# Far groups' softmax sums with a constant column, an early load of the softplus table, and another order up to the first MLP's end

## Chip, cores, metric

The kernel runs on one core of one Trainium2 chip. The metric is the device time of one execution in microseconds. For a profiled execution the span is also known: the time from the program's first instruction to its last.

## What is computed

Three stages follow each other: attention in a window of 64 positions, a softplus MLP, and a gated MLP.

```python
batch, n_heads, seq, head_dim = (4, 8, 576, 64)
scores = scale * np.matmul(q, k.transpose(0, 1, 3, 2))
mask = (rel >= 0) & (rel < window)          # rel = pos[:, None] - pos[None, :], window = 64
scores = np.where(mask, scores, -1000000000.0)
attn = np.exp(scores - np.max(scores, axis=-1, keepdims=True))
attn = attn / (np.sum(attn, axis=-1, keepdims=True) + 1e-09)
x = np.matmul(attn, v)                      # to 2304 tokens x 512
h = x @ w_in                                # 512 x 2048
g = np.maximum(h, 0.0) + np.log1p(np.exp(-np.abs(h)))
x = g @ w_out                               # 2048 x 512
gate = 1.0 / (1.0 + np.exp(-(x @ w_gate)))  # 512 x 1536
out = (gate * (x @ w_val)) @ w_out2         # 1536 x 512
```

The weights and the second MLP's input come as 64-bit numbers and are used as pairs of rounded fp32 parts, a high and a low one; so are all activations that enter a matmul.

## The kernel before

**Groups.** The 2304 tokens are cut into 36 groups of 64 queries. For each, `att_scores` multiplies queries and keys on TensorE, `att_max` (VectorE) takes each row's maximum, `att_exp` (ScalarE, line 381) the exponential with a running sum of each row, `att_sum` (VectorE, lines 384 to 390) adds 1e-9 to the sums and takes the reciprocal, `att_norm` (GpSimd, line 397) multiplies, and then the result is transposed (on TensorE, lines 409 and 413, or for later groups by VectorE and DMAs) and multiplied with the values (`att_values`, line 474). `att_hi` (ScalarE, line 482) and `att_lo` (VectorE, line 487) write the high and low part of the attention output into the first MLP's input `xt`. Groups 0 to 7 are called near: they run before the first MLP starts, and are block 0. Groups 8 to 35 are far: they run while the first MLP works on the block before theirs.

**Sums.** In a near group the exponential's running sum goes into the first of two columns of a tile `sums` whose second column was set to 1e-9, and one `tensor_reduce` over the two columns adds it. In a far group it goes into the group's statistics tile `st`, and a `tensor_scalar` adds 1e-9:

```python
        if g < NG0:
            nc.vector.tensor_reduce(out=st[:, 1, :], in_=sums[:, g], axis=AX.X, op=ALU.add)
        else:
            nc.vector.tensor_scalar(out=st[:, 1, :], in0=st[:, 1, :], scalar1=1e-9, scalar2=None, op0=ALU.add)
```

**The first MLP, M1.** Five blocks of 512, 384, 384, 512 and 512 tokens; in each, 16 steps f. `m1_proj(b, f)` (line 514, 12 matmuls) projects into one of two PSUM banks h0 and h1. `m1_act` (ScalarE, line 531) is the softplus, in place. `g_hi` (ScalarE, line 538) and `g_lo` (VectorE, line 544) write its high and low part; after `g_lo` the bank is free, and `m1_proj(b, f + 2)` may use it. `m1_out(b, f)` (lines 491 to 493, 12 matmuls) adds into four other banks, two steps behind. In the text "the first projection" is `m1_proj(0, 0)`, "the third" `m1_proj(0, 2)`, and so on. The first two projections use all high parts first. ScalarE needs one table of functions for the exponential and another one for softplus; a load of a table stands in the program where the next activation needs another one than the last (`ACT_TABLE_LOAD`).

**Weights.** While block 0 runs, the first MLP's weights are turned from 64 bits into pairs, tile by tile: `w_load` (a DMA on SyncE's queue), `w_scale` (ScalarE, lines 175 and 177), `w_shift`, `w_sign`, `w_low` (VectorE, lines 181, 186, 191), `w_hi` (ScalarE, line 197) and `w_lo` (VectorE or GpSimd, line 205). Tiles 0 and 1 are the first two projections' weights; from tile 2 on, two tiles are scaled together. With the exponential's table in, `w_scale` uses another function (line 175), and `w_sign` isn't needed.

**The order.** All steps up to the first MLP's end are put into one list by a planner, `lead_in` (lines 1080 to 1167). Each step has an engine, a cost in us, the steps it depends on and a due time (`traits`, lines 903 to 1057, and lines 1082 to 1106). The planner keeps a time for each engine, and takes, again and again, from the steps that can start soonest (within `NEAR` or `SLACK`) the one that is due first. The numbers at the file's head steer it: `LATE` and `STAY` hold a visit of the attention on TensorE back or keep visits of a kind together, `SWITCH` and `FLIP` price a change of ScalarE's table, `FETCH` and `PAUSE` model the DMAs, `RG` spaces the near groups, `OPEN` is the planned start of the first MLP, `COMBO0` the slot at which the second MLP's weights are first prepared. The list fixes the order of instructions on every engine, the DMA queue of SyncE among them. What comes after the first MLP (lines 1178 to 1180) has an order of its own.

Of the kernel before, what the change touches and what calls it, by code (L numbers as in the profile page):

```python
# [10 lines left out]
F32 = mybir.dt.float32  # L11
# [3 lines left out]
AF = mybir.ActivationFunctionType  # L15
ALU = mybir.AluOpType
AX = mybir.AxisListType
# [3 lines left out]
P = 128  # L21
# [1 line left out]
HALF = 384  # L23
LAG = 2
LEAD = 7
COMBO0, COMBO = 37, 10.0
FAR = 2
MERGE = 8
SHIFTED = 2,
RG = 1.2  # L30
HURRY = 1.5
SLACK, NEAR = 0.1, 0.2
STAY = 10.0
FETCH, PAUSE, SAFE = 15.5, 1.4, 0.4
OPEN = 30.0
FLYING, SWITCH, MARGIN, FLIP, LATE = 10, 1.3, 1.1, 8, 0.5
EITHER, HALVES = (("pool", 1.29), ("dve lock", 0.69)), (("pool", 0.75), ("dve lock", 0.42))
COPIES = ("act", 0.55), ("dve", 0.69)
LO_AT = ((5, 2), (6, 6), (8, 9), (9, 12), (13, 15), (15, 18), (19, 21))
# [13 lines left out]
def tile_kernel(ctx: ExitStack, tc: tile.TileContext, qk, vt, w1, w2, wg, wv, wo, out):  # L53
# [20 lines left out]
    nc = tc.nc  # L74
# [19 lines left out]
    main = ctx.enter_context(tc.tile_pool(name="main", bufs=2))  # L94
# [6 lines left out]
    early = main.tile([P, 2, DM], BF16, tag="sums", name="early", bufs=1)  # L101
    ident16, mask16 = (early[:, k, :P] for k in range(2))
    sums = early[:, 0, P:2 * P].bitcast(F32).rearrange("p (g j two) -> p g j two", j=4, two=2)
    x2d = dram.tile([KC, P, NT], F32, tag="x2d", name="x2d")
    wcd = [dram.tile([P, 14 * HC], F32, tag=f"wcd{f}", name=f"wcd{f}") for f in range(NF2)]
    pd = [dram.tile([4, 32, 4, P], F32, tag=f"pd{i}", name=f"pd{i}") for i in range(2)]
# [155 lines left out]
    NG0 = BLOCKS1[0] // Q  # L262
# [107 lines left out]
    def att_bias(g, engine):  # L370
        t = st_t[g][:, 0, :]
        eng = nc.gpsimd if engine == "pool" else nc.vector
        eng.tensor_scalar(out=t, in0=t, scalar1=SCALE, scalar2=None, op0=ALU.mult)

    def att_exp(g):
        w = width(g)
        p, st = p_t[g], st_t[g]
        s, scale = ([p[:, j] for j in range(NPAIR)], 1.0) if g >= NG0 else (
            [s_t[g][:, h, j] for h in range(s_t[g].shape[1]) for j in range(NPAIR // s_t[g].shape[1])], SCALE)
        for j in range(NPAIR):  # L380
            nc.scalar.activation(out=p[:, j, :w], in_=s[j][:, :w], func=AF.Exp, bias=st[:, 0, j:j + 1], scale=scale,  # L381
                                 accum_out=sums[:, g, j, :1] if g < NG0 else st[:, 1, j:j + 1])

    def att_sum(g):
        st = st_t[g]
        if g < NG0:
            nc.vector.tensor_reduce(out=st[:, 1, :], in_=sums[:, g], axis=AX.X, op=ALU.add)
        else:
            nc.vector.tensor_scalar(out=st[:, 1, :], in0=st[:, 1, :], scalar1=1e-9, scalar2=None, op0=ALU.add)
        nc.vector.reciprocal(out=st[:, 2, :], in_=st[:, 1, :])  # L390

    def att_norm(g):
# [135 lines left out]

    def m1_act(b, f):
        t = h_t.pop((b, f))  # L530
        nc.scalar.activation(out=t, in_=t, func=AF.Softplus)  # L531
        u_t[b, f] = t

# [254 lines left out]
    for b in range(1, NB1):  # L788
        s0, s1 = pos[m1_proj, b - 1, 0], pos[m1_proj, b, 0]
        ng, g0 = BLOCKS1[b] // Q, starts1[b] // Q  # L790
        for j in range(ng):
            far = b >= FAR
            first = -5 if far else 5
            t = s0 + first + (s1 - s0 - (14 if far else 12 + first)) * (j // 2) // max(ng // 2 - 1, 1)
            attention(g0 + j, t, far)
            at(t - 4, -60, qk_load, g0 + j)

# [21 lines left out]
    for f in range(NF2):  # L819
        t, i = COMBO0 + int(COMBO * f), len(seq1) + 2 * f  # L820
# [12 lines left out]
    for f in range(NF2):  # L833
        i = WO_AT + f
        t = end + (-7, -1)[f] if f < 2 else pos[m2_out, 0, f - 2, 0] - 1
# [33 lines left out]

    def consts():  # L870
        nc.gpsimd.memset(sums, 1e-9)
        make_identity(nc, ident)
        nc.vector.tensor_copy(out=ident16, in_=ident)
        for t, inside, outside in (mask16, 0.0, -1e30), (mask, 3.0e38, -1e9):
            nc.gpsimd.memset(t, inside)
            for h in range(2):
                m = t[h * Q:(h + 1) * Q, :]
                nc.gpsimd.affine_select(out=m, in_=m, pattern=[[1, P]], compare_op=ALU.is_ge, fill=outside, base=-1,
                                        channel_multiplier=-1)
                nc.gpsimd.affine_select(out=m, in_=m, pattern=[[-1, P]], compare_op=ALU.is_ge, fill=outside, base=Q,  # L880
                                        channel_multiplier=1)
# [198 lines left out]
    def lead_in():  # L1080
# [30 lines left out]
        while todo:  # L1111
            ready, other = [], "soft" if table == "exp" else "exp"
            for n, key in enumerate(todo[:AHEAD]):
# [5 lines left out]
                if all(d in done for d in deps + after[key]):  # L1119
                    ends_at, best = [(done[d] - lead(key, d), made[d]) for d in deps], None  # L1120
                    visit = kind == "pe" and key[0] not in (m1_proj, m1_out) and key[1] >= NG0
                    for kind, us in kind if kind in CHOICES else ((kind, us),):
                        engine, *need = kind.split()
                        start = max([t - (0.08 if e == "pe" else 0.05) * (e == engine) for t, e in ends_at], default=0.0)
                        start = max(free[engine], start + LATE * visit)
                        if engine == "pool" or "lock" in need:
                            start = max(start, held["dve" if engine == "pool" else "pool"])
                        if engine == "sp" and len(flying) >= FLYING:
                            start = max(start, flying[-FLYING])
                        if engine == "act" and need and need[0] != table:  # L1130
                            us += SWITCH
                        if best is None or start + us < best[0] + best[2]:
                            best = start, kind, us
# [97 lines left out]
```

## Time and profile before

| | |
|---|---|
| time, median of 3 runs (range) | 878.88 us (878.85 to 881.1) |
| profiled execution | 878.93 us, its span 877.1 us |
| TensorE matmuls, busy | 868.3 us (99%) |
| TensorE weight loads, busy | 775.3 us (88%) |
| VectorE, ScalarE, GpSimd, busy | 519.4 us (59%), 395.5 us (45%), 151.1 us (17%) |
| 16 DMA engines | 202 GB/s to and from HBM over the span |

An engine's busy time counts its instructions from start to end; matmuls overlap and their ends are modelled. The engines wait for each other by semaphores, and each takes its own instructions strictly in order, so an instruction that waits holds up all behind it on its engine.

### The profile page before, as it was taken

Reading aid. Unit: us, or ns where it says so; the run is one execution under the profiler, and the core shown is the slowest. Engines: PE = TensorE matmul, PEld = TensorE weight load, DVE = VectorE, ACT = ScalarE, POOL = GpSimd, SP = SyncE. Lnnn points to the kernel's source line nnn. Section 1 sums busy time; section 2 is a strip of 40 time slices with the busy share of each in tenths; the row PEclk is TensorE's granted clock in tenths of the full one; section 3 lists DMA queues with packets and bytes.
Section 4 is the critical chain, followed back from the end, with each engine's and each line's share of the span. In section 5 each row is a group of like instructions: output and inputs, shape, how many; then the busy total and the mean of one; then the engine's idle time right before and its main releaser. Section 6 shows DMA issues by size and latency. Waiting matters only on the chain.

```text
span 877.1 us, 14033 instructions
## 1 busy us (share of the span) xinstructions
PE 868.3 (99%) x5307; PEld 775.3 (88%) x5307; DVE 519.4 (59%) x926; ACT 395.5 (45%) x870; POOL 151.1 (17%) x156
## 2 busy tenths in 40 slices
PE   8999999999999999999999999999999999999998
PEld 5787889999999888888889999999999999999997
DVE  5999985547665654555326677667444448444444
ACT  7878766556566763344323333343222225212222
POOL 5001110112000220012002232332111111111110
PEclk9999999999999999999999999999999999999999
DMA  9955647756877747643325755546554445444442
GB/s 363 390 181 207 207 143 269 246 207 211 263 254 261 266 150 269 199 165 132 133 84 208 269 207 216 217 168 240 208 200 160 151 150 209 168 158 168 169 168 73
DMA packets 56563, 177.73 MB, mean 203 GB/s; under 512 B 6128, under 2 KB 21744, under 8 KB 51888
## 3 DMA queue, kind: packets, MB, share of 16 engines
q1 hardware_dynamic: 56496, 176.84, 56.4%
q8 instruction: 42, 0.69, 0.3%
q14 instruction: 25, 0.20, 0.1%
HBM read 139.59 MB, written 37.22 MB: 202 GB/s over the span
## 4 chain that ended last, share of the span: by engine, by line
PE 93%; ACT 3%; DVE 3%; issue 1%; DMA 1%; POOL 0%; SPq 0%; POOLq 0%; DVEq 0%; ACTq 0%
PE h L514 21%; PE acc L491 11%; PE acc L492 11%; PE acc L493 11%; PE h L491 10%; PE h L493 10%; PE h L492 10%; PE at L493 2%; PE at L492 2%; PE at L491 2%; PE at L474 2%; PE at L335 1%; ACT w L381 1%; DMA w<-in_qk 1%; DVE w L186 1%
## 5 line engine op out<-in xcount | busy, mean ns | idle before, releaser
L514 PE MATMUL h<-xt,w 128*128 128x512 f32 (+1 forms) x960 | 211.6, 369 | 0.9 <-DVE g L544 0.7
L620 DVE TENSOR_TENSOR w<-h,w 128x384 f32<-128x384 f32 x216 | 117.1, 556 | 159.9 <-PE h L493 157.0
L514 PEld LDWEIGHTS h<-xt,w 128*128 128x128 f32 x960 | 174.2, 188 | 25.6 <-DVE g L544 0.9
L491 PE MATMUL h<-w,wc 128*128 128x384 f32 x504 | 169.1, 336 | 0.1
L493 PE MATMUL h<-w,wc 128*128 128x384 f32 x504 | 168.9, 335 | 0.0
L492 PE MATMUL h<-w,wc 128*128 128x384 f32 x504 | 168.7, 335 | 0.0
L632 POOL TENSOR_TENSOR g<-w,g 128x384 fp32r<-128x384 f32 x70 | 74.0, 1057 | 297.0 <-ACT g L625 252.1
L491 PE MATMUL acc<-g,w 128*128 128x512 f32 (+1 forms) x320 | 119.4, 373 | 0.0
L492 PE MATMUL acc<-g,w 128*128 128x512 f32 (+1 forms) x320 | 117.7, 368 | 0.0
L493 PE MATMUL acc<-g,w 128*128 128x512 f32 (+1 forms) x320 | 117.7, 368 | 0.0
L544 DVE TENSOR_TENSOR g<-h,g 128x512 fp32r<-128x512 f32 (+1 forms) x80 | 50.8, 636 | 93.9 <-ACT g L538 87.5
L531 ACT ACTIVATE h<-h 128x512 f32<-128x512 f32 (+1 forms) x80 | 43.0, 540 | 124.2 <-PE h L514 122.2
L491 PEld LDWEIGHTS h<-w,wc 128*128 128x128 f32 x504 | 94.6, 188 | 2.7 <-DVE w L620 0.7
L492 PEld LDWEIGHTS h<-w,wc 128*128 128x128 f32 x504 | 94.6, 188 | 2.0
L493 PEld LDWEIGHTS h<-w,wc 128*128 128x128 f32 x504 | 94.6, 188 | 0.0
L625 ACT CAST g<-w 128x384 fp32r<-128x384 f32 x72 | 36.9, 513 | 118.6 <-DVE w L620 118.6
L491 PEld LDWEIGHTS acc<-g,w 128*128 128x128 f32 x320 | 60.1, 188 | 8.9 <-issue 1.0
L493 PEld LDWEIGHTS acc<-g,w 128*128 128x128 f32 x320 | 60.1, 188 | 7.6
L492 PEld LDWEIGHTS acc<-g,w 128*128 128x128 f32 x320 | 60.1, 188 | 7.1
L397 POOL TENSOR_TENSOR p<-p,st 128x512 f32<-128x512 f32 x28 | 30.7, 1099 | 201.0 <-DVE st L390 114.4
L658 ACT ACTIVATE w<-w 128x384 f32<-128x384 f32 x36 | 19.0, 527 | 94.5 <-DVE w L620 94.4
L493 PE MATMUL acc<-w,g 128*128 128x512 f32 x144 | 56.9, 395 | 0.0
(138 smaller groups left out, 1187.6 us busy)
## 6 DMA issues: line engine op xcount, KB each, us to landing
wc<-wcd SPq DMA_DIRECT2D x36, 1792.0 KB, 7.3
qk<-in_qk SPq DMA_DIRECT2D x28, 512.0 KB, 5.5
wcd<-raw SPq DMA_DIRECT2D x24, 512.0 KB, 3.2
w<-in_w SPq DMA_DIRECT2D x16, 512.0 KB, 8.8
raw<-in_w SPq DMA_DIRECT2D x16, 512.0 KB, 4.9
v<-in_vt SPq DMA_DIRECT2D x25, 256.0 KB, 3.2
raw<-in_wg SPq DMA_DIRECT2D x12, 512.0 KB, 5.3
raw<-in_wv SPq DMA_DIRECT2D x12, 512.0 KB, 6.2
```

The costliest lines, as they stand in the source:

```text
L397: nc.gpsimd.tensor_tensor(out=p[:, j:j + n, :w], in0=p[:, j:j + n, :w], in1=st[:, 2, j:j + n].unsqueeze(2).to_broadcast([P, n, w]), op=ALU ...
L474: nc.tensor.matmul(out=o[h * Q:(h + 1) * Q, j, k * Q:(k + 1) * Q], lhsT=v[r, (2 * j + h) * Q:(2 * j + h + 1) * Q], rhs=pt, start=True, sto ...
L491: nc.tensor.matmul(out=o, lhsT=lh, rhs=rh, start=first, stop=False)
L492: nc.tensor.matmul(out=o, lhsT=lh, rhs=rl, start=False, stop=False)
L493: nc.tensor.matmul(out=o, lhsT=ll, rhs=rh, start=False, stop=last)
L514: nc.tensor.matmul(out=o, lhsT=w[:, i, kc * P:(kc + 1) * P], rhs=x[:, j, kc, :n], start=t == 0, stop=t == len(turns) - 1)
L531: nc.scalar.activation(out=t, in_=t, func=AF.Softplus)
L544: nc.vector.tensor_tensor(out=g[:, 1, :n], in0=t, in1=g[:, 0, :n].bitcast(F32), op=ALU.subtract)
L620: nc.vector.tensor_tensor(out=out, in0=a, in1=b, op=op)
L625: nc.scalar.copy(out=g[:, 0, :HALF], in_=t)
L632: eng.tensor_tensor(out=g[:, 1, :HALF], in0=t, in1=g[:, 0, :HALF].bitcast(F32), op=ALU.subtract)
L658: nc.scalar.activation(out=sb, in_=u2, func=AF.Sigmoid)
```

## The change

Three things are changed. The far groups' running sums go into a new tile `far_sums` of three rows (group g uses row g mod 3) with a second column of 1e-9, and all groups take their sum by `tensor_reduce`. The softplus table is asked for by an instruction of its own ahead of the first softplus. The planner's numbers are other ones; it counts on 0.135 us instead of 0.05 by which a step may start before its forerunner on the same engine is done, and gives the first softplus a start that is earlier by `SWITCH`; visits in the first MLP's blocks are due at slightly other slots.

```diff
-COMBO0, COMBO = 37, 10.0
+COMBO0, COMBO = 36, 10.0
-RG = 1.2
+RG = 1.0
-SLACK, NEAR = 0.1, 0.2
-STAY = 10.0
-FETCH, PAUSE, SAFE = 15.5, 1.4, 0.4
-OPEN = 30.0
-FLYING, SWITCH, MARGIN, FLIP, LATE = 10, 1.3, 1.1, 8, 0.5
+SLACK, NEAR = 0.1, 0.1
+STAY = 30.0
+FETCH, PAUSE, SAFE = 12.8, 1.4, 0.4
+OPEN = 35.0
+FLYING, SWITCH, MARGIN, FLIP, LATE = 10, 1.3, 1.1, 10, 1
...
+    far_sums = main.tile([P, 3, 4, 2], F32, tag="far_sums", name="far_sums", bufs=1)
...
+    def sum_row(g):
+        return sums[:, g] if g < NG0 else far_sums[:, g % 3]
+
...
-                                 accum_out=sums[:, g, j, :1] if g < NG0 else st[:, 1, j:j + 1])
+                                 accum_out=sum_row(g)[:, j, :1])
...
-        if g < NG0:
-            nc.vector.tensor_reduce(out=st[:, 1, :], in_=sums[:, g], axis=AX.X, op=ALU.add)
-        else:
-            nc.vector.tensor_scalar(out=st[:, 1, :], in0=st[:, 1, :], scalar1=1e-9, scalar2=None, op0=ALU.add)
+        nc.vector.tensor_reduce(out=st[:, 1, :], in_=sum_row(g), axis=AX.X, op=ALU.add)
...
+        if b + f == 0:
+            nc.scalar.preload_act_table(AF.Softplus)
         nc.scalar.activation(out=t, in_=t, func=AF.Softplus)
...
-            first = -5 if far else 5
-            t = s0 + first + (s1 - s0 - (14 if far else 12 + first)) * (j // 2) // max(ng // 2 - 1, 1)
+            first = -5 if far else 6
+            t = s0 + first + (s1 - s0 - (15 if far else 12 + first)) * (j // 2) // max(ng // 2 - 1, 1)
...
         nc.gpsimd.memset(sums, 1e-9)
+        nc.gpsimd.memset(far_sums, 1e-9)
...
-                        start = max([t - (0.08 if e == "pe" else 0.05) * (e == engine) for t, e in ends_at], default=0.0)
-                        start = max(free[engine], start + LATE * visit)
+                        start = max([t - (0.08 if e == "pe" else 0.135) * (e == engine) for t, e in ends_at], default=0.0)
+                        start = max(free[engine], start + LATE * visit - SWITCH * (key == (m1_act, 0, 0)))
```

What it does to the order is shown at three places, in the names of the program: `xt` is the first MLP's input, `bits` and `w` are weights, `h` a projection's bank, `g` the parts of its softplus. Line numbers of the changed kernel are higher by one to four.

ScalarE at the end of the near groups, before: the casts of groups 6 and 7 are the row with x2, and the first softplus is the row before the last.

```order
L482 CAST xt<-at 128x4x64
L197 CAST w_481<-bits 128x512
L443 COPY pt<-s_473 128x256
L175 ACTIVATE bits<-w_154 128x512
L482 CAST xt<-at 128x4x64 x2
L175 ACTIVATE bits<-w_255 128x1024
L197 CAST w_481<-bits 128x512
L175 ACTIVATE bits<-w_289 128x1024
L531 ACT_TABLE_LOAD
L531 ACTIVATE h_523<-h_523 128x512
L197 CAST w_566<-bits 128x2x512
L538 CAST g<-h_523 128x512
```

The same place now:

```order
L483 CAST xt<-at 128x4x64
L198 CAST w_483<-bits 128x512
L444 COPY pt<-s_475 128x256
L176 ACTIVATE bits<-w_156 128x512
L483 CAST xt<-at 128x4x64
L176 ACTIVATE bits<-w_257 128x1024
L483 CAST xt<-at 128x4x64
L198 CAST w_483<-bits 128x512
L176 ACTIVATE bits<-w_327 128x1024
L533 ACT_TABLE_LOAD
L534 ACTIVATE h_529<-h_529 128x512
L541 CAST g<-h_529 128x512
```

The scaling of weight tiles 2 and 3 (128x1024) moved between the casts of groups 6 and 7, the table load belongs to a line of its own, and the g cast moved ahead of a weight cast.

VectorE from the low half of weight tiles 4 and 5 on, before:

```order
L191 SCALAR_TENSOR_TENSOR bits<-w_289,bits 128x1024
L205 TENSOR_TENSOR w_566<-bits,w_566 128x512
L544 TENSOR_TENSOR g<-h_523,g 128x512
L205 TENSOR_TENSOR w_566<-bits,w_566 128x512
L205 TENSOR_TENSOR w_592<-bits,w_592 128x512 x2
```

and now:

```order
L192 SCALAR_TENSOR_TENSOR bits<-w_327,bits 128x1024
L547 TENSOR_TENSOR g<-h_529,g 128x512
L206 TENSOR_TENSOR w_571<-bits,w_571 128x512 x2
L365 SCALAR_TENSOR_TENSOR p<-at,mask 128x256
L364 MEMSET p 128x2x64
```

The subtraction for the first projection's g (`g_lo`) moved ahead of the low part of weight tile 2, and the maximum of group 8 follows the tiles 2 and 3.

ScalarE around the exponentials of groups 8 and 9, before (the fourth projection's softplus is the third row, the fifth one's the last):

```order
L177 ACTIVATE w_619<-raw 128x1024
L197 CAST w_670<-bits 128x2x512
L531 ACTIVATE h_650<-h_650 128x512
L381 ACT_TABLE_LOAD
L381 ACTIVATE p,st<-p,st 128x128 x4
L538 CAST g<-h_650 128x512
L381 ACTIVATE p,st<-p,st 128x128 x4
L197 CAST w_717<-w_619 128x2x512
L531 ACT_TABLE_LOAD
L531 ACTIVATE h_693<-h_693 128x512
```

and now:

```order
L178 ACTIVATE w_670<-w_508 128x1024
L534 ACTIVATE h_651<-h_651 128x512
L541 CAST g<-h_651 128x512
L178 ACTIVATE w_670<-w_566 128x1024
L198 CAST w_714<-w_627 128x2x512
L385 ACT_TABLE_LOAD
L385 ACTIVATE p,far_sums<-p,st 128x128 x8
L198 CAST w_760<-w_627 128x2x512
L534 ACT_TABLE_LOAD
L534 ACTIVATE h_692<-h_692 128x512
```

The exponentials moved behind the fourth projection's g cast and behind the scaling of tiles 12 and 14 (the two rows with w_670), which stood after the fifth softplus before. On TensorE the transposes of groups 8 and 9 moved from behind `m1_out(0, 4)` to ahead of the seventh projection, and the scores of groups 10 and 11 from behind the eighth projection to ahead of it; the transposes of groups 10 and 11 stand behind one `m1_out` more.

## Rows read from the trace of the kernel before

**Rows 1.** The page, part 1: busy us, share of the span, instructions.

```profile
PE 868.3 (99%) x5307; PEld 775.3 (88%) x5307; DVE 519.4 (59%) x926; ACT 395.5 (45%) x870; POOL 151.1 (17%) x156
```

**Rows 2.** Stretches: PE, PEld, DVE, ACT, POOL busy us (instructions); PEclk, DMA share, GB/s.

```profile
28.00:80.00 52.00, 50.67 (x310) 40.97 (x309) 49.62 (x75) 43.50 (x79) 4.93 (x4) 1.00 0.75 273
80.00:160.00 80.00, 80.00 (x584) 70.06 (x584) 63.15 (x104) 53.95 (x116) 8.53 (x8) 1.00 0.57 195
```

**Rows 3.** Order of time, TensorE, 23.5 to 35: start, us, instruction, [idle before <-releaser].

```profile
24.18 0.82 PE L504 MATMUL s<-idle 128*128 128x512 bf16 x2
25.14 0.70 PE L514 MATMUL h<-xt,w 128*128 128x512 f32 x2
...
30.77 0.90 PE L335 MATMUL at<-qk 64*64 64x128 f32 x32
32.41 2.79 PE L514 MATMUL h<-xt,w 128*128 128x512 f32 x11 [0.74 <-DVE g L544]
```

**Rows 4.** Order of time, TensorE, 59.5 to 77.

```profile
59.75 1.03 PE L413 MATMUL at<-ident,p 128*128 128x128 f32 x8
60.54 3.18 PE L514 MATMUL h<-xt,w 128*128 128x512 f32 x12
63.65 0.56 PE L335 MATMUL at<-qk 64*64 64x128 f32 x12
...
74.47 0.60 PE L413 MATMUL at<-ident,p 128*128 128x128 f32 x4
75.66 0.66 PE L413 MATMUL at<-ident,p 128*128 128x128 f32 x4 [0.59 <-POOL p L397]
76.07 1.18 PE L514 MATMUL h<-xt,w 128*128 128x512 f32 x4
```

**Rows 5.** The chain of work that ended last: start, us, engine and line.

```profile
81.79 2.72 PE h L514 x12
...
153.62 0.83 PE at L335 x32
...
321.32 2.94 PE h L514 x12
```

**Rows 6.** Order of time, ScalarE, 21.5 to 33.

```profile
24.00 0.65 ACT L482 CAST xt<-at 128x256 fp32r<-128x256 f32 x2
24.55 1.16 ACT L175 ACTIVATE bits<-w 128x1024 f32<-128x1024 f32 x1
...
28.20 1.28 ACT L531 ACT_TABLE_LOAD   x1 [0.52 <-PE h L514]
29.49 0.58 ACT L531 ACTIVATE h<-h 128x512 f32<-128x512 f32 x1
...
30.92 0.59 ACT L538 CAST g<-h 128x512 fp32r<-128x512 f32 x1
```

**Rows 7.** Order of time, VectorE, 24 to 33.

```profile
28.99 1.23 DVE L191 SCALAR_TENSOR_TENSOR bits<-w,bits 128x1024 uint32<-128x1024 uint32 x1
31.06 0.69 DVE L205 TENSOR_TENSOR w<-bits,w 128x512 fp32r<-128x512 f32 x1 [0.84 <-ACT w L197]
31.67 0.68 DVE L544 TENSOR_TENSOR g<-h,g 128x512 fp32r<-128x512 f32 x1
```

**Rows 8.** Order of time, VectorE and GpSimd, 71 to 77.5.

```profile
73.17 1.01 DVE L389 TENSOR_SCALAR st<-st 128x4 f32<-128x4 f32 x1
...
72.31 1.84 POOL L397 TENSOR_TENSOR p<-p,st 128x512 f32<-128x512 f32 x1 [19.91 <-DVE st L390]
```

**Rows 9.** Lines 389 and 387: count, duration min/median/max in ns, first and last start.

```profile
L389 DVE TENSOR_SCALAR st<-st x28: 126/170/1008, 49.8 to 323.9; 128x4 f32<-128x4 f32 x28
...
L387 DVE TENSOR_REDUCE st<-early x8: 130/150/161, 7.4 to 19.3; 128x4 f32<-128x8 f32 x8
```

**Rows 10.** SyncE's queue in order of time; page, part 6: issues, KB, us to landing.

```profile
32.87 1.56 SPq L146 DMA_DIRECT2D w<-in_w  x2
...
w<-in_w SPq DMA_DIRECT2D x16, 512.0 KB, 8.8
```

## The prediction

> **What bounds the kernel now.** I read the page's busy shares first. TensorE's matmuls fill 99% of the span, VectorE 59%, ScalarE 45% [rows 1]. A busy matmul row need not mean a matmul engine at its peak, so next come the sums by stretch. From 28 to 80 us TensorE has 50.67 us of work in 52, so 1.33 us are idle, while VectorE is busy for 49.62 of the 52. From 80 to 160 us TensorE has no gap at all (80.00 of 80) and VectorE has 17 us to spare [rows 2]. TensorE's order of time names both gaps of the first stretch in its brackets: 0.74 us before a projection of the first MLP (line 514), ended by VectorE's line 544 [rows 3], and 0.59 us before transposes (line 413), ended by GpSimd's line 397 [rows 4]; together they are the 1.33. The reader is to see that everything after 80 us is a full queue on TensorE: the change can gain only where that queue starts, or where it has holes before 80 us. In the full queue a step of 12 matmuls with 512 columns takes 2.72 us, or 2.94 behind a visit of the attention's small matmuls; a visit of scores with half-width tiles takes 0.83 [rows 5].
>
> **Term 1, the first projection starts later.** In the kernel before, ScalarE casts the rounded attention output of groups 6 and 7 one behind the other (line 482, 24.00 for 0.65 us, so it ends at 24.65), and then scales weight tile 2 (1.16 us) [rows 6]. TensorE's two idle matmuls, 24.18 for 0.82 us, end at 25.00, and the first projection starts at 25.14 [rows 3]. It was held by the idle matmuls, not by the casts. In the changed order the scaling of tile 2 stands between the two casts. The second cast, 0.37 us long by the end of the pair, moved from a start at 24.28 to 24.28 + 1.16 - 0.10 = 25.34 (neighbours on ScalarE overlap by about 0.1 us: the scaling starts at 24.55, the casts end at 24.65 [rows 6]). It ends at 25.71. All first matmuls read all eight groups' columns, so they start some 0.14 us later (the distance from the idle matmuls' end to the projection's start [rows 3]), at 25.85: **+0.71 us**. It would be 0 if values of group 7 were the later input in both, and +1.16 if nothing overlapped. I take 0.71, since the order leaves no other way.
>
> **Term 2, the wait of 0.74 us goes.** Before, the third projection needs the bank of the first one. The chain is: table load 28.20 to 29.48, softplus 29.49, a weight cast, the g cast 30.92 of 0.59 us [rows 6], then VectorE's subtraction, which starts at 31.67 behind another one and takes 0.68 us [rows 7]. The projection starts at 32.41, although the scores before it (30.77, then 0.90 us with the last ones' modelled ends) left TensorE at 31.67 [rows 3]. Now the load stands ahead of softplus' wait: it can run when tile 4's scaling is done. That one waits for its weights and ended 0.52 us before 28.20, at 27.68, so the load is over at 28.96. The first projection ends at 25.85 + (28.20 - 25.14) = 28.91, softplus runs 28.97 to 29.55, the g cast, now ahead of the weight cast, to 30.1, and VectorE, whose longer step of 28.99 + 1.23 ends at 30.2 [rows 7], subtracts until 30.9. TensorE gets there after two projections and the scores: 25.85 + (30.77 - 25.14) + 0.83 = 32.31. So the bank is free 1.4 us early and the wait is gone. The third projection starts at 32.31 instead of 32.41: **-0.10 us**, terms 1 and 2 together. Load and swapped casts each save about 1 us on a chain of which 0.74 was needed; the scores then are what ends last.
>
> **Term 3, a stretched projection.** At 60.54 a projection takes 3.11 us until the scores at 63.65 [rows 4]. Behind a visit in the full queue it takes 2.94 [rows 5]. What stretched it is the low half of its weights, which VectorE finishes at about the same time. In the new order the transposes of groups 8 and 9 come one projection earlier and the scores ahead of this projection, and VectorE has its idle time at 30.2 to 31.06 [rows 7] behind it. I take 2.94 - 3.11 = **-0.17 us**; bounds 0, and -0.39 against the 2.72.
>
> **Term 4, the transposes of groups 10 and 11.** They take 76.07 - 74.47 = 1.60 us, those of groups 8 and 9 took 60.54 - 59.75 = 0.79 [rows 4]: 0.81 us are lost. The cause stands on VectorE and GpSimd. The `tensor_scalar` of line 389 that adds 1e-9 took 1.01 us from 73.17, until 74.17; GpSimd's multiplication began at 72.31 and ended at 74.15 [rows 8]. The median of that sum is 170 ns [rows 9]. The two engines exclude each other there. The same sum in the near groups is a `tensor_reduce` with the constant in a second column, at 150 ns, never above 161 [rows 9]. The change gives the far groups that form. In that place it saves 0.85 us of VectorE, and elsewhere time that VectorE has to spare. The transposes also stand behind one more m1_out now. I take **-0.81 us**; bounds 0 (GpSimd's own work still ends last) and -0.9.
>
> The Trainium skill speaks against this step: VectorE: DVE Perf Modes (The perf-mode tier table) says that `tensor_reduce` has only the 1x rate, while `tensor_scalar` in fp32 has 2x. By that rule each of the 28 sums would get dearer by a few ns, and the four that lie before 80 us would add less than 0.1 us to the sum. The row is measured with eight elements against four and shows 20 ns less [rows 9], so the sum goes by it.
>
> **Costed at nothing.** The new memset of 128x24 on GpSimd is smaller than a mask; the identity and masks that follow are ready long before the first scores need them. Without that cover it would cost some 0.15 us. The exponentials write 1e-9's neighbour in a ring of three rows, so group g's wait for the sum of g - 3: that sum lies a whole visit back, and would cost one sum (0.15 us) if not. Four sign steps fewer on VectorE (tiles scaled while the exponential table is in) lie after 65 us, where VectorE gains room and TensorE nothing. On SP, loads of queries for groups 12 and 13 move ahead of two weight loads and values 10 and 11 behind two others; a load needs 8.8 us from issue to landing in the crowded start [rows 10], and their users are at least two slots of 5.4 us away. The visits of attention on TensorE are as many as before (31), each with the same borders.
>
> **Sum.** -0.10 - 0.17 - 0.81 = -1.08 us, from 878.93 us of the profiled execution (span 877.1 and 1.8 around it) to **877.8 us** (877.85). The median of the three runs shown, 878.88, is the same within 0.05 us.
>
> **Rivals.**
> 1. The start isn't delayed: something else (the values of group 7, the idle matmuls) still ends last, or the cast slips in earlier. Then all waits go: -0.74 - 0.17 - 0.81, 877.2 us. Against it stands the order, which puts 1.16 us between two casts.
> 2. The waits only change place: the transposes or a low half end last again. 878.9 us. For it speaks VectorE's 49.62 of 52 us [rows 2]: it is the real supply of this stretch, and a queue that starts at the same time asks for its weights just as early.
> 3. Slower: the exponentials of groups 8 and 9 now stand behind the scaling of tile 14. Its loads are issued at 32.87 to 34.4 and take 8.8 us [rows 10], so they land at 43.2 or later, while ScalarE is through with the g cast of the fourth projection at about 42.3: it idles up to 1.5 us, and table, exponentials, weight casts and the softplus of the fifth projection are all behind it. By my walk the bank that the seventh projection needs comes free 0.8 us before TensorE asks. From the point at which that slack is used up, each us late is a us lost. With the whole 1.5 us lost at that place and terms 3 and 4 not gained: 878.9 - 0.1 + 1.5 = 880.3 us. Two such places: 881.8 us.
> 4. The change doesn't do what it says: a load still stands behind softplus' wait. Then softplus is 1.28 us later, the bank is free at 32.2, still before 32.31. The time is 877.8 all the same; it only shows in the trace.
> 5. TensorE's matmuls are not the bound before 80 us. Its weight loads fill 88% of the span [rows 1] and 40.97 of the 52 us [rows 2]; if these set the pace, 11 us of the stretch were open to a better order, 867 us. The Trainium skill, Perfetto Trace Analysis (Identifying the Most-Contended Engine), judges TensorE by that row and not by matmul time. Against it stands the constant 2.72 us for 12 matmuls wherever nothing is waited for [rows 5]: a faster supply would not shorten these.
>
> **How the numbers follow.** Forecast with rival 4: 0.53. Rival 1: 0.15. Rival 2: 0.10. Rival 3 with one place 0.13, with two or more 0.07. Rival 5: 0.02. No change that can be told apart by a measurement of this kernel is about 0.3%, 2.6 us: below 876.2 is faster, above 881.5 slower. Faster needs rival 5, or rival 1 and as much again at the start: 0.04. Slower needs two places of rival 3 or more: 0.08. The rest, 0.88, is no difference. The range takes in the forecast with its bounds, rivals 1 and 2 and one place of rival 3: 876.8 to 880.4.
>
> **What would show it.** Right: the first projection at about 25.85, a table load of line 533 that ends before 29 us with no wait for TensorE ahead of it, no wait of line 515 for 547 at 32 us, no sum above 0.2 us on VectorE, transposes of groups 10 and 11 in 0.8 us. Wrong: the projection at 25.1 (rival 1); new waits of TensorE before 80 us, ended by VectorE or ScalarE, above all at the seventh projection (rivals 2 and 3); any gap after 80 us.

## The result

| | before | changed |
|---|---|---|
| time, median | 878.92 us (878.85 to 881.1, 4 runs) | 891.25 us (890.61 to 891.78, 4 runs) |
| profiled execution, span | 878.93, 877.1 us | 890.78, 888.9 us |

The changed kernel is slower: the ratio is 1.0135, with a 95% interval of 1.0119 to 1.0151. Forecast were 877.8 us and a range from 876.8 to 880.4.

The page of the changed kernel, part 1, in the columns of [rows 1]:

```profile
PE 880.2 (99%) x5307; PEld 778.9 (88%) x5307; DVE 514.8 (58%) x922; ACT 397.2 (45%) x871; POOL 151.4 (17%) x156
```

TensorE has as many matmuls as before (5307) and is as full (99%), but busy for 11.9 us more. The other engines have hardly more to do: ScalarE is busy for 1.7 us more, GpSimd for 0.3, VectorE for 4.6 less. So the time is not in a wait; the matmuls themselves have become slower. The stretches of [rows 2]:

```profile
28.00:80.00 52.00, 52.00 (x309) 41.48 (x308) 47.23 (x72) 43.57 (x78) 5.27 (x4) 1.00 0.73 260
80.00:160.00 80.00, 80.00 (x581) 69.22 (x580) 57.21 (x97) 53.49 (x115) 9.82 (x9) 1.00 0.59 203
```

The 1.33 us of gaps before 80 us are gone, as forecast. But a full queue now gets through 581 matmuls from 80 to 160 us where it got through 584, at the same granted clock of 1.00 (2.4 GHz). (The order of the attention's small matmuls is another one. In e8 below, with the changed order and the old addresses, the same stretch has 598.) TensorE's order of time shows the start, as in [rows 3]:

```profile
24.41 0.82 PE L505 MATMUL s<-idle 128*128 128x512 bf16 x2
25.96 5.87 PE L515 MATMUL h<-xt,w 128*128 128x512 f32 x24 [0.72 <-ACT xt L483]
31.76 0.90 PE L336 MATMUL at<-qk 64*64 64x128 f32 x32
32.59 2.60 PE L515 MATMUL h<-xt,w 128*128 128x512 f32 x10
```

and ScalarE's the steps that the forecast had walked through, as in [rows 6]:

```profile
24.50 1.15 ACT L176 ACTIVATE bits<-w 128x1024 f32<-128x1024 f32 x1
25.55 0.36 ACT L483 CAST xt<-at 128x256 fp32r<-128x256 f32 x1
...
28.00 1.28 ACT L533 ACT_TABLE_LOAD   x1
29.30 0.58 ACT L534 ACTIVATE h<-h 128x512 f32<-128x512 f32 x1
29.91 0.59 ACT L541 CAST g<-h 128x512 fp32r<-128x512 f32 x1
```

The first projection starts at 25.96 us (forecast 25.85), held by group 7's cast; the table is in at 29.28 (forecast 28.96); the third projection starts at 32.59 without a wait. The loss is in the pace. The chain of waits (start, us, engine and line) in block 4 of the first MLP, before:

```profile
389.44 2.72 PE h L514 x12
394.88 2.72 PE h L514 x12
```

and the changed kernel:

```profile
395.52 2.80 PE h L515 x12
401.12 2.80 PE h L515 x12
```

A projection of 12 matmuls with 512 columns takes 2.80 us where it took 2.72 [rows 5]; the table below has the pace of all large matmuls. The first product of the second MLP in TensorE's order of time shows how the loss is spread, before (line 491) and then changed (line 492):

```profile
454.55 0.33 PE L491 MATMUL h<-w,wc 128*128 128x384 f32 x1
```

```profile
462.56 0.34 PE L492 MATMUL h<-w,wc 128*128 128x384 f32 x1
```

8.0 us are lost until there, and 888.9 - 462.56 - (877.1 - 454.55) = 3.8 behind it, where the change edits nothing.

### The profile page after: what moved, and what is told of

Its sections match the earlier page's. It is cut to its first block, busy times and chain, and to the rows that moved or that the text cites. A ratio compares the mean times of both kernels' runs of the same rounds, so it can differ in the third digit from the quotient of the medians.

```text
span 888.9 us, 14028 instructions
## 1 busy us (share of the span) xinstructions
PE 880.2 (99%) x5307; PEld 778.9 (88%) x5307; DVE 514.8 (58%) x922; ACT 397.2 (45%) x871; POOL 151.4 (17%) x156
## 4 chain that ended last, share of the span: by engine, by line
PE 97%; ACT 1%; DMA 1%; DVE 0%; POOL 0%; SPq 0%; issue 0%
PE h L515 23%; PE acc L492 12%; PE acc L494 11%; PE acc L493 11%; PE h L492 10%; PE h L494 10%; PE h L493 10%; PE at L494 2%; PE at L492 2%; PE at L493 2%; PE at L475 2%; PE at L336 2%; ACT w L385 1%; DMA w<-in_qk 1%; PE at L414 0%; ACT xt L483 0%
## 5 line engine op out<-in xcount | busy, mean ns | idle before, releaser
L515 PE MATMUL h<-xt,w 128*128 128x512 f32 (+1 forms) x960 | 216.9, 375 | 0.7 <-ACT xt L483 0.7
L492 PE MATMUL acc<-g,w 128*128 128x512 f32 (+1 forms) x320 | 120.4, 376 | 0.0
L494 PE MATMUL acc<-g,w 128*128 128x512 f32 (+1 forms) x320 | 119.3, 373 | 0.0
L493 PE MATMUL acc<-g,w 128*128 128x512 f32 (+1 forms) x320 | 118.8, 371 | 0.0
```

The lines of the kernel that those rows point to most:

```text
L492: nc.tensor.matmul(out=o, lhsT=lh, rhs=rh, start=first, stop=False)
L493: nc.tensor.matmul(out=o, lhsT=lh, rhs=rl, start=False, stop=False)
L494: nc.tensor.matmul(out=o, lhsT=ll, rhs=rh, start=False, stop=last)
L515: nc.tensor.matmul(out=o, lhsT=w[:, i, kc * P:(kc + 1) * P], rhs=x[:, j, kc, :n], start=t == 0, stop=t == len(turns) - 1)
```

## The experiments

**The theory.** The one thing that the change does to all of the program is to place tiles. `far_sums` has 3 x 4 x 2 numbers of 4 bytes in each partition, 96 bytes, and is allocated in the pool `main` behind `early`. All tiles of `main` behind it, and the pools behind `main`, move up by 96 bytes: `xt`, `g`, `g2`, `wc` (the second MLP's weights) and the attention's small tiles. The weights' slots w0 to w15, in which the second MLP's input parts lie too, are in a pool ahead of it and stay. In the program before, the slots, xt, wc and g all begin 128 bytes behind a multiple of 256. Theory A is that these addresses set the pace. Rival B is that the order, the sums or the table load do.

A matmul has two operands. The stationary one (`lhsT` in the kernel) is what the weight load reads; the moving one is the other. In the first MLP the stationary operand is a w slot and the moving one `xt` or `g`.

The measurements are the times and, from each trace, the mean distance from one large matmul's start to the next one's, in ns. It is taken only where another large matmul follows, and without the distances that are over a quarter longer than the rest (at most 15 of some 570 in a column). "Proj" and "out" are the first MLP's `m1_proj` and `m1_out`, with 512 and 384 columns; "prod" and "last" the second MLP's products (384 columns; moving: a w slot, stationary: wc) and its last matmuls (512; moving: a w slot, stationary: g2):

```
                              proj 512  out 512  proj 384  out 384  prod   last
before                          227.4    227.5    173.7    173.5   174.2  229.3
changed                         233.4    233.3    176.7    176.7   174.9  233.8
e1  changed, far_sums away      227.7    227.2    173.5    173.6   174.2  229.3
e2  before, 96 bytes            233.3    233.4    176.7    176.7   174.0  233.8
e3  before, 64 bytes            229.0    229.1    173.4    173.4   176.7  233.4
e4  before, 32 bytes            233.2    233.2    174.4    174.4   173.7  233.2
e6  before, all by 32           227.4    227.5    173.7    173.5   174.2  229.3
e13 before, g and g2 by 96      229.7    234.2    175.0    176.6   174.7  233.9
e14 before, wc by 192           227.4    227.5    173.7    173.5   173.5  229.1
e15 before, wc by 64            227.4    227.6    173.6    173.5   174.7  229.4
```

**e1: the change without the shift.** Only the place of `far_sums` is another; of all tiles only the attention's small ones stay shifted:

```diff
-    far_sums = main.tile([P, 3, 4, 2], F32, tag="far_sums", name="far_sums", bufs=1)
+    far_sums = None
...
     def consts():
+        nonlocal far_sums
+        far_sums = late["apool"].tile([P, 3, 4, 2], F32, tag="far_sums", name="far_sums", bufs=1)
```

> The changed kernel with its order, its sums and its early table load, but the tile far_sums (96 bytes per partition) is taken from the pool of the attention's small tiles instead of from the pool main, so that xt, wc, g, g2 and raw lie again where they lay in the kernel before (addresses that are multiples of 128 bytes); only the attention's small tiles stay shifted by 96 bytes. Theory A (the 12 us come from the shifted addresses of what TensorE's large matmuls read): 877 to 879.5 us, a projection of 12 matmuls with 512 columns 2.72 us again. Rival B (the new order, the sums or the early load slow TensorE): 890 to 892 us, a projection 2.80 us.

Measured: 879.02 us (ratio to before 1.0004, 0.9995 to 1.0013). The chain of this kernel has the old pace:

```profile
389.05 2.72 PE h L515 x12
394.49 2.72 PE h L515 x12
```

**e2 to e4: the shift without the change.** The kernel before, with a tile in the place of `far_sums` (24, 16 or 8 numbers):

```diff
+    pad = main.tile([P, 24], F32, tag="pad", name="pad", bufs=1)
...
         nc.gpsimd.memset(sums, 1e-9)
+        nc.gpsimd.memset(pad, 1e-9)
```

> The kernel before with nothing changed but a tile of 96 bytes per partition behind early in the pool main, set once by GpSimd and never read. Theory A: the loss of the change and not its gain of about 1 us, so 890.5 to 892.5 us, a projection with 512 columns 2.80 us. Rival B: 878.9 us, 2.72 us.

> The kernel before with a tile of 64 bytes in that place: every address behind it leaves 64 over a multiple of 128. Theory A says that the shift counts, not from which step on: if multiples of 64 are good enough 878.9 us, if it must be 128 then 885 to 892 us. Rival B: 878.9 us.

> The kernel before with a tile of 32 bytes in that place. Theory A: if multiples of 64 or of 128 are wanted, 890 to 892.5 us as with 96 bytes; if multiples of 32 are good enough (then 96 bytes would do no harm either) 878.9 us. Rival B: 878.9 us.

Measured: 889.72 us with 96 bytes (1.0118, 1.0103 to 1.0134), 886.72 with 64 and 886.98 with 32 (both 1.0089, 1.0075 to 1.0103). Theory A holds and B falls: a tile that nothing reads costs 10.5 us, the changed kernel without the shift nothing. The 96 bytes came out 0.8 us under the lower end of what was expected, and the 32 bytes 3.0 us under the 890 expected for a loss. Part of the first may lie in the products: at the same addresses they take 174.0 ns in e2 and 174.9 in the changed kernel, and why is open. The chain of waits of the kernel with 96 bytes (e2), then with 64 (e3):

```profile
395.93 2.80 PE h L515 x12
401.53 2.80 PE h L515 x12
```

```profile
390.31 2.75 PE h L515 x12
395.81 2.75 PE h L515 x12
```

**e6: all operands by the same 32 bytes.** Is it each address by itself, or how the two operands of a matmul lie to each other? Here a pad stands ahead of everything, the weights included:

```diff
+    pad = const.tile([P, 8], F32, tag="pad", name="pad")
     ident = const.tile([P, P], F32, tag="ident", name="ident")
```

> The kernel before with a tile of 32 bytes ahead of everything, so that the weights move by 32 bytes as well: moving and stationary operands of every large matmul leave 32 over a multiple of 128. Theory A1 (each operand's own address counts): no better than the 886.98 us of the shift by 32 bytes that left the weights in place; 886.5 to 891 us, matmuls with 512 columns 233 ns apart. Theory A2 (what counts is how the two operands lie to each other): 878.9 to 879.5 us, 227 ns apart.

Measured: 878.89 us (0.9998, 0.9988 to 1.0007), where 32 bytes without the weights gave 886.98. So the distance between the two operands counts, not the address. The chain of this kernel has the old pace:

```profile
389.37 2.72 PE h L515 x12
394.81 2.72 PE h L515 x12
```

**e7 and e10: which distances.** Views into tiles that have room give other offsets from step to step, here for g2 in e7:

```diff
+    SHIFTS_X, SHIFTS_W = (0, 8, 16, 24, 4, 12, 32), (0, 8, 16, 24, 4, 32)
...
-        g = main.tile([P, 2, NMAX], F32R, tag="g", name="g2", bufs=GB)
+        d = SHIFTS_W[f % 6]
+        g = main.tile([P, 2, NMAX], F32R, tag="g", name="g2", bufs=GB)[:, :, d:d + HALF]
```

> The kernel before; in the second MLP the input's parts lie 0, 32, 64, 96, 16, 48 and 128 bytes behind a multiple of 128, one offset for each of the seven products, and the weights wc and the parts g2 lie 0, 32, 64, 96, 16 and 128 bytes behind, one offset for each f mod 6; in blocks 1 and 2 of the first MLP g lies so too. Every operation is kept. So each pair of offsets of moving and stationary operand is seen in one trace. Theory A1: the products (384 columns) are slower by 1 to 4 ns in all columns of the table where the moving operand is off, whatever the weights' offset; the last products (512 columns, g2 stationary) are 229 ns at offsets 0 and 128 and 233 ns elsewhere if a stationary operand counts too. Theory A2: the cells with equal offsets stay at the 174 ns of the kernel before. Both: 879.5 to 884 us.

> The kernel before with larger offsets, every operation kept: g2, the stationary operand of the second MLP's last products (512 columns), lies 256, 512, 384, 320, 448, 288, 480, 192, 160, 224, 416 and 352 bytes off for f = 0 to 11, wc up to 2048 bytes off, and in blocks 1 and 2 of the first MLP g lies 32 bytes times f off. Theory A2 (how the two operands lie to each other counts, with a period): 227 to 229 ns again at 512 bytes or already at 256, 229 to 236 ns elsewhere; were any offset faster than 227 ns, a layout with it would beat both kernels. Rival A3 (only equal positions in the tile's own start count, no period): 229 to 236 ns at 512 too. The time: 881 to 885 us.

Measured: 882.76 and 882.31 us. The last matmuls, whose moving operand stays in its place, by the offset of g2 (mean distance in ns between matmuls of the same step; 229.4 in the kernel before):

```
bytes   0      16     32     64     96     128    160    192    224
e7      226.7  232.4  233.3  233.5  233.6  232.6
e10                                               233.4  229.1  233.3
bytes   256    288    320    352    384    416    448    480    512
e10     229.1  233.1  232.9  233.9  232.0  233.3  229.1  233.0  229.1
```

The period is 256 bytes: 256 and 512 are alike, and so is each offset from 32 to 224 and the one 256 bytes behind it, within 0.6 ns. At 0, 192, 256, 448 and 512 the pace is that of the kernel before or better (e7's 226.7, behind products with other distances; why is not shown), and everywhere else it is 232 to 234. The first MLP fits, with its moving operand shifted: 64 bytes there are a stationary operand 192 behind (229.0 and 229.1), 96 are 160 (233.3 and 233.4), 32 are 224 (233.2 and 233.3). No offset went clearly below 227 ns. e7's table of the products, some 30 matmuls to a cell, gave values from 172.5 to 178.6 without a plain pattern. Equal offsets (174.0 to 177.1) are no better than others, where 174 had been expected of them; a step's neighbours have other distances there, so the table bears out nothing, and for the products the rule rests on e14 and e15. e10's larger offsets of wc, 173.3 to 176.4 ns, do not settle it either.

**e13: g and g2 off by 96 bytes.** A pad behind `xt` in the kernel before; of what the large matmuls read, only g and g2 move (`raw`, `bits` and the attention's small tiles move too):

```diff
             xt_t[b] = main.tile([P, 2, KC, NMAX], F32R, tag="xt", name="xt", bufs=2)
+            if b == 0:
+                nc.gpsimd.memset(main.tile([P, 24], F32, tag="pad", name="pad", bufs=1), 1e-9)
```

> The kernel before with a tile of 96 bytes between xt and raw: xt, wc and the weights lie as before, g and g2 are off by 96 bytes. Theory A2: projections stay at 227 ns, the first MLP's output matmuls go to 233 ns (384 columns: 177), the second MLP's products stay at 174.3, its last products go to 233.8. 576 x 6.6 + 384 x 3.4 + 648 x 4.4 ns = 8 us: 886.5 to 887.5 us. Rival (shifting any tile slows the whole engine): projections at 233 ns too, 889 us or more.

Measured: 888.87 us (1.0116, 1.0099 to 1.0132), 1.4 us over the range. The outputs went to 234.2 ns and the last matmuls to 233.9 as expected, but the projections, whose operands had not moved, to 229.7. Within a projection of blocks 3 and 4 the first eight mean distances lie between 225 and 235 ns, the last four at 226.6 to 226.7: a step starts in the manner of the step before it and needs some eight matmuls to come back. The rival is not it (that would be 233 to the end); the time alone, 0.1 us under the rival's 889, could not have told them apart.

**e14 and e15: wc alone.** The edit of e14; e15 has 16 for 48:

```diff
-        t = main.tile([P, 14 * HC], F32R, tag="xt", name="wc", bufs=2)
+        t = main.tile([P, 14 * HC + 48], F32R, tag="xt", name="wc", bufs=2)[:, 48:]
```

> The kernel before with wc, the stationary operand of the second MLP's products, 192 bytes behind its place (distance 192 from the moving operand, no operation changed). Theory A2 with the sign (192 is one of the good distances): the products go from 174.3 to 173.3 ns, 1512 x 1.0 ns = 1.5 us, and 877.4 us; if the last products, which follow them, also gain (229.4 to 227 ns, 648 of them), 876 us. Rival (the step in the mixed run came from its neighbours): 878.5 to 880 us.

> The same with 64 bytes. Theory A2 with the sign: 176.8 ns a product, as in the run with all tiles but the weights 64 bytes off, 1512 x 2.5 ns = 3.8 us, 882 to 883.5 us. Rival (only the distance without its sign counts, 64 is as good as 192): 877 to 879 us.

Measured: 878.1 us with 192 bytes (0.9988, 0.9979 to 0.9997) and 879.48 with 64 (1.0004, 0.9995 to 1.0013). The products go to 173.5 and 174.7 ns, so the sign counts. The sizes were over-rated: 1512 x 0.7 = 1.1 us gained instead of 1.5, and 1512 x 0.5 = 0.8 lost instead of 3.8. The 176.7 ns of e3 came at the same 64 bytes with g2 and the other tiles off as well; which of these it takes was not tried. Nor is distance 0 the best one for the products: before has 174.2 ns at 0, e4 173.7 at 32 and e2 174.0 at 96.

**The parts of the change, with the addresses restored.** e8 has `far_sums` in a pool of its own at the end of the memory, so that no tile moves. e9 also puts the cast of group 7 ahead of the scaling of tiles 2 and 3. e11 is the kernel before with the new sums alone, e12 the new order alone, e17 the early load alone (the two lines of the change).

```diff
-    far_sums = main.tile([P, 3, 4, 2], F32, tag="far_sums", name="far_sums", bufs=1)
+    far_sums = None
...
         late["apool"] = apool_cm.__enter__()
+        far_sums = fpool_cm.__enter__().tile([P, 3, 4, 2], F32, tag="far_sums", name="far_sums", bufs=1)
```

> The changed kernel with far_sums behind the attention's small tiles, at the end of the memory, so that every tile lies where it lay in the kernel before. Theory A: 877 to 878.5 us, the 1 us that the forecast saw in the order; if the attention's small tiles, which were off by 96 bytes in the first experiment, cost what that one lacks to this, 0.5 to 1 us below its 879.02. Rival (the rest is given back by the order itself in blocks 1 to 4): 879 us again.

> The last one, and the cast of group 7's attention output stands ahead of the scaling of weight tiles 2 and 3 again, as in the kernel before. By the forecast's first term the first projection starts 0.7 us earlier (25.2 us instead of 25.9), and the time is 0.7 us below that of the last experiment. Rival: the weights of the third projection then come late and it starts no earlier; the same time.

> The kernel before with the far groups' sums taken by the reduction over a constant column, far_sums at the end of the memory so that nothing else moves; its own order and table load. By the forecast's fourth term the sum of group 10 or 11 takes 0.15 us instead of 1.01, the transposes 0.8 instead of 1.6 us, block 1 starts up to 0.8 us earlier and the time is 878.1 to 878.4 us. Rival: GpSimd's own work ends last all the same, 878.9 to 879.1 us.

> The changed kernel's order alone, with the old sums and without the early table load; no tile far_sums, so every address is that of the kernel before. Theory A: no trace of the 12 us, 878 to 879.6 us; softplus starts 1.3 us later than in the changed kernel and the third projection still starts at about 32.5 us without a wait; the sum by tensor_scalar may meet GpSimd's work again, up to 0.9 us. Rival B (the order itself costs the 12 us): 890 us.

> The kernel before with the early load of the softplus table alone. By the forecast's second term softplus is over 1.2 us earlier and the wait of 0.74 us ahead of the third projection goes: it starts at 31.7 us, block 1 starts 0.7 us earlier and the time is 878.2 to 878.6 us. Rival (the low half of the weights, which waited too, comes late and takes its place; or the 0.7 us are waited for later): 878.9 to 879.1 us.

| | time, us | ratio to before (95%) | start of block 1, us |
|---|---|---|---|
| before | 879.08 | | 120.37 |
| e11, sums alone | 879.1 | 1.0006 (0.9996 to 1.0015) | 120.32 |
| e17, early load alone | 878.49 | 0.9993 (0.9984 to 1.0003) | 120.02 |
| e12, order alone | 879.21 | 1.0003 (0.9994 to 1.0012) | 119.64 |
| e8, the whole change | 878.68 | 0.9991 (0.9982 to 1.0000) | 119.18 |
| e9, and the cast first | 878.83 | 0.9995 (0.9986 to 1.0004) | 118.85 |

The last column is the start of the first 384-column projection in TensorE's order of time. Before, then e8:

```profile
120.37 2.27 PE L514 MATMUL h<-xt,w 128*128 128x384 f32 x12
```

```profile
119.18 2.27 PE L515 MATMUL h<-xt,w 128*128 128x384 f32 x12
```

Up to block 1 the change is worth 1.2 us. By these intervals none of the five times is sure to differ from before. But the ten runs of e17 (878.39 to 878.67 us) all lie below the thirty-three of before beside them (878.83 to 881.26), so its 0.6 us are likely real. Each ratio is to the runs of before beside it (medians 879.01 to 879.09). e9 was expected 0.7 us below e8 and is not: its first projection starts 0.68 us earlier, its block 1 only 0.33. What became of e8's 1.2 us its list of waits tells (engine and line, what was waited for: us in total, times, longest):

```profile
PE at L475 <- DMA pt<-pd: 1.0, 1, 1.0
PE h L515 <- ACT xt L483: 0.7, 1, 0.7
```

In block 2 TensorE waits for 1.0 us for probabilities that are transposed by way of DMAs. Before has no such wait, nor have e9 and e1 in their profiled executions; e16 below has one of 0.7. The times of e8 spread over 2.5 us (877.44 to 879.92); that this wait comes and goes would fit, but only one execution has a trace. e11 shows where the sums' part went. GpSimd's second multiplication in the kernel before, then VectorE and GpSimd in e11, in order of time as in [rows 8]:

```profile
74.56 1.04 POOL L397 TENSOR_TENSOR p<-p,st 128x512 f32<-128x512 f32 x1 [0.41 <-DVE st L390]
```

```profile
73.11 0.16 DVE L387 TENSOR_REDUCE st<-far_sums 128x4 f32<-128x8 f32 x1
```

```profile
72.25 3.30 POOL L395 TENSOR_TENSOR p<-p,st 128x512 f32<-128x512 f32 x2 [19.89 <-DVE st L388]
```

The sum takes 0.16 us instead of 1.01 and is done while GpSimd multiplies. GpSimd's second multiplication now follows the first without a gap, but the two take 3.30 us instead of 1.84 and 1.04, so it ends at 75.55 instead of 75.60. TensorE still waits for it, by the list of e11's waits:

```profile
PE h L512 <- DVE g L542: 0.7, 1, 0.7
PE at L411 <- POOL p L395: 0.6, 1, 0.6
```

**e16: a version that beats both.** e9 with wc 192 bytes behind its place.

> The changed kernel with far_sums at the end of the memory, the cast of group 7 ahead of the scaling of tiles 2 and 3, and wc 192 bytes behind its place. If e14 gains its 1.5 us: 877.3 us, below both kernels; if e14 gains nothing: 878.8 us as without the shift.

Measured: 877.62 us (0.9984, 0.9975 to 0.9993), 1.5 us under the kernel before and 13.6 under the changed one; 0.3 us from what was expected. Its second MLP starts at 454.09 us in a span of 875.3, so it takes 421.2 us instead of 422.6; the first 0.5 us less than before.

## Why the prediction was wrong

**The step that failed** is the sentence "In the full queue a step of 12 matmuls with 512 columns takes 2.72 us", which was carried over to the changed kernel as if it belonged to the matmul, together with "Costed at nothing", which priced the new tile by its memset alone. Its place was not looked at. By the table the first MLP loses 576 x 6.0 + 576 x 5.8 ns with 512 columns and 384 x 3.0 + 384 x 3.2 with 384, 9.2 us in all. The gain at the start leaves 8.0 of these. The second MLP loses 1512 x 0.7 + 648 x 4.5 = 4.0 us (3.8 measured). The 0.7 ns a product, 1.1 us of that, are not shown to come from the addresses, since e2 has none of them at the same ones. The chances given to the forecast and its rivals add up to 1, and all of them move only waits, or let matmuls be faster: a slower matmul had no place among them.

**Term 1, the later start.** Right: 25.96 for 25.85, with the cast of group 7 as the releaser. e9 takes the delay back; its TensorE in order of time:

```profile
25.05 5.69 PE L515 MATMUL h<-xt,w 128*128 128x512 f32 x24
30.67 0.90 PE L336 MATMUL at<-qk 64*64 64x128 f32 x32
31.49 2.78 PE L515 MATMUL h<-xt,w 128*128 128x512 f32 x11
```

**Term 2, the wait ahead of the third projection.** Right: no wait, 32.59 us, and 32.22 with the old pace in e8 (forecast 32.31). The forecast let the load and the swapped casts each save about 1 us. The load alone does less; in e17 0.47 us of the 0.74 are still waited for, since the weight cast still stands ahead of the g cast, and the low part of that weight ahead of VectorE's subtraction. Its TensorE in order of time:

```profile
32.06 3.02 PE L514 MATMUL h<-xt,w 128*128 128x512 f32 x12 [0.47 <-DVE g L546]
```

Rival 4 was not needed: the load is over at 29.28. With the old load, in e12, the third projection starts at 32.41 and does not wait either, as rival 4 had said.

**Term 3, the stretched projection.** Not tried by itself. In the changed kernel this projection follows a visit, runs at the new pace, and 62.69 to 65.60 us is 2.91 (forecast 2.94), less than the 3.11 of before [rows 4]:

```profile
62.69 3.07 PE L515 MATMUL h<-xt,w 128*128 128x512 f32 x12
65.60 0.40 PE L492 MATMUL acc<-g,w 128*128 128x512 f32 x1
```

**Term 4, the transposes of groups 10 and 11.** The size came out and the cause did not. They take their 0.8 us in the changed kernel, where they stand one `m1_out` later:

```profile
81.02 1.04 PE L414 MATMUL at<-ident,p 128*128 128x128 f32 x8
81.81 3.05 PE L515 MATMUL h<-xt,w 128*128 128x512 f32 x12
```

The forecast laid this to the sums; e11 shows that the sums alone save 0.85 us of VectorE and nothing of TensorE, because GpSimd's own work ends last. That was the term's bound of 0. The order did it: e12, with the old sums, has no such wait either. The far sums are short now, with a median of 161 ns (170 before) and a largest one of 164, as forecast from [rows 9]; but that is VectorE's time, of which this place had enough.

**The sum and the rivals.** -1.08 us was right up to block 1 (-1.19 in e8). Behind it a new wait of rival 2's kind took 1.0 us of it back in the profiled execution of e8. Without the shift the time would have been e8's 878.7 us (879.0 in e1), inside the range. None of the rivals had the mechanism. Rival 5 came nearest to it, in doubting that matmul time is a property of the matmul alone; but it expected a gain and gave it 0.02. Rival 3 did not come about: TensorE has no gap between 28 and 80 us.

## What to carry to other kernels

A new small tile moves every tile behind it. Where TensorE is full, compare the start addresses of the operands of the large matmuls before and after an edit, as well as the instructions, and put small tiles at the end of the memory (e8), or, by the period and not tried by itself, fill them up to 256 bytes; when a busy engine gets busier with the same instructions, compare one step's duration in the full queue first.

## What the runs showed of the hardware

The distance modulo 256 bytes between the addresses of moving and stationary operand sets the pace of fp32 matmuls that follow each other without a gap. With 512 columns they are 227 to 229 ns apart at 0 and 192, and 232 to 234 at the other distances tried; with 384 columns the first MLP's are 173.5 apart at 0 and up to 176.7 elsewhere, and the second MLP's products do not follow the same table (174.2 at 0, 173.5 at 192). With both operands moved by the same 32 bytes nothing happens. The runs show the distance, its period, its sign, and that a disturbed step still disturbs the first eight matmuls of the next one. What meets what inside TensorE they do not show; that the load of the next weights meets the running matmul's reads is a guess. The mean duration of a weight load, 188 ns in both kernels, tells nothing of it, as the page's costliest groups show, before and then changed (busy us, mean ns of one):

```profile
L514 PE MATMUL h<-xt,w 128*128 128x512 f32 (+1 forms) x960 | 211.6, 369 | 0.9 <-DVE g L544 0.7
...
L514 PEld LDWEIGHTS h<-xt,w 128*128 128x128 f32 x960 | 174.2, 188 | 25.6 <-DVE g L544 0.9
```

```profile
L515 PE MATMUL h<-xt,w 128*128 128x512 f32 (+1 forms) x960 | 216.9, 375 | 0.7 <-ACT xt L483 0.7
...
L515 PEld LDWEIGHTS h<-xt,w 128*128 128x128 f32 x960 | 174.5, 188 | 28.8 <-issue 1.7
```

The Trainium skill, TensorE: Matmul & The Clock Gate (Step-by-step: what each phase is for), says that TensorE has two independent read ports into SBUF and that loading the next tile's weights takes no read bandwidth from the running matmul. Of where the operands lie it says nothing there. e6 against e4, 878.89 against 886.98 us with the same instructions, shows that placement changes the pace all the same; whether it does so by the weight loads, against that rule, or in another way, no run here shows.
